# mLSTM cell and leaky-ReLU MLP on one core: the first weight matrix loaded slot by slot, onto 128 partitions at a time

## The chip, the cores and the metric

The kernel runs on one core of a Trainium2 chip. The metric is device time in microseconds (us) of one execution of the whole program. Inputs lie in the chip's memory (HBM) at the start, and the output has to be there at the end. The core has a matrix engine (PE, with PEld for the weight loads that overlap it), a vector engine (DVE), an activation engine (ACT), GpSimd (POOL) and a sync engine (SP). Each works through its own list of instructions in order, and they wait for one another on semaphores. Sixteen DMA engines move data between HBM and the on-chip memory (SBUF, 128 partitions); loads are issued from the queues of SP and ACT.

## The reference

Two stages. The first is an mLSTM cell with gates over 4 batches, 8 heads, 768 time steps and a head size of 40; the second is an MLP with a leaky ReLU on its 3072 rows of 320 numbers:

```python
for t in range(S):
    m_new = np.maximum(f_gate[:, :, t] + m, i_gate[:, :, t])
    f_stab = np.exp(f_gate[:, :, t] + m - m_new)
    i_stab = np.exp(i_gate[:, :, t] - m_new)
    C = f_stab[:, :, None, None] * C + i_stab[:, :, None, None] * np.einsum('bhd,bhe->bhde', vt, kt)
    n = f_stab[:, :, None] * n + i_stab[:, :, None] * kt
    h_tilde = np.einsum('bhde,bhe->bhd', C, qt)
    y[:, :, t] = o * h_tilde / np.maximum(np.abs((n * qt).sum(-1)), 1.0)[:, :, None]
...
x = attn_out.transpose(0, 2, 1, 3).reshape(B * S, H * D)   # 3072 x 320
h = x @ w_in                                               # 320 x 2048
return np.maximum(0.01 * h, h) @ w_out                     # 2048 x 320
```

(The line of `y` joins three of the reference's.) The two weight matrices are 64-bit floating-point numbers, so a row of w_in is 2048 x 8 = 16 KB in HBM, and 256 of its columns are 2 KB. Everything else is 32-bit.

## The kernel before, in words

**Chunks and units.** Time is cut into 6 chunks of 128 steps. For each chunk there are four steps, one for each batch, numbered `s` (0 to 3 are chunk 0). The cell of a chunk is worked out on all engines and gives x transposed (`xT`); the MLP of that chunk is cut into units (`ff_units`) that are laid between the cell's units of the next chunk. The orders of PE, DVE, ACT and POOL are written out by hand (`tc.manual_schedule`); SP's order is left to a scheduler.

**Chunk 0.** `first_chunk` issues the first loads and works through the cell of chunk 0. Then the main loop runs over the 32 units of chunk 0's MLP (`i` counts them) with the cell of chunk 1 between them. The first 16 units (L763, tile `ph`) multiply with w_in, the other 16 (L785, tile `po`) with w_out. The first eight of them use quarters 0 and 1 of w_in, the next eight quarters 2 and 3.

**w_in in SBUF.** The 320 rows of w_in are five blocks of 64, and its 2048 columns are four quarters of 512. A quarter (`n`) holds two sets of 256 columns, `r` = 0 and 1. Set 0 lies on partitions 0 to 63, set 1 on partitions 64 to 127, so that two matmuls of 64 rows can stand side by side. On each half the five blocks stand in five slots of 256 columns, in an order of its own:

```python
SLOTS = ([0, 2, 4, 1, 3], [1, 3, 0, 2, 4])
```

so slot 0 holds block 0 on the lower half and block 1 on the upper half, slot 1 blocks 2 and 3, slot 2 blocks 4 and 0, slot 3 blocks 1 and 2, slot 4 blocks 3 and 4.

**Loading and narrowing.** `load_weights(n)` loads quarter `n` as raw 64-bit words (L234): quarters 0 and 1 into the tail of the tile `acts`, 2 and 3 into the tile `raw`. For `n` of 4 and more it loads a pair of w_out's row blocks (L241). `narrow_weights(n)` then turns the words into 32-bit numbers in six steps: two on ACT (L253, L254) and four on DVE (L255, L258, L261, L262). L253 is the first to read the raw words. A quarter is usable when L262 has run.

Before, a quarter is loaded by four transfers. `run_of` finds the runs of slots whose blocks are two apart: three and two slots on the lower half, two and three on the upper. Each transfer writes 64 partitions, and its pattern has the 64 rows outermost, then two or three blocks, then 256 columns.

**What stands around the loads.** On SP's queue: k, q and v of steps 0 and 1 (L365), quarter 0, the output gates of steps 0 and 1, gates of chunk 2 (L94, L95), k and q of steps 2 and 3, quarter 1, v and output gates of steps 2 and 3, then a store to `a_dr` (L312), k and q for step 4 (L350, L377), quarters 2 and 3, v of step 4 (L354), and the tile `w` of step 4, two broadcast loads from `a_dr` (L407). Step 4 is the first of chunk 1. On it, POOL adds a mask to `w` (`prep_mask`, L446), POOL scales q (L483), ACT takes the exponent of `w` (`prep_exp`, L454), and PE turns the scaled q (`split_qs`, tile `tq`, L527) at unit 6 of the MLP. ACT's rows at L771 are the leaky ReLU of a unit; they free the PSUM banks that the unit wrote. From chunk 1 on, x goes through HBM: `u_mix` stores it to `x_dr` by four transfers of 20 partitions (L720), and `gather_x` loads it back (L734).

Every DMA announces its landing on one of eight semaphores, used in turn, and an issue waits for the earlier transfer on its semaphore.

Of the kernel before, what the change touches and what calls it, by code (L numbers as in the profile page):

```python
# [18 lines left out]
def kernel(  # L19
# [26 lines left out]
    nc = tc.nc  # L46
    B, H, S, D = q.shape
    P = 128
# [3 lines left out]
    Dm, FF = moe_w_in.shape  # L52
    PR = H // 2
    DP = 64
# [13 lines left out]
    KC = Dm // DP  # L68
    SLOTS = ([0, 2, 4, 1, 3], [1, 3, 0, 2, 4])
# [93 lines left out]
    QC = 4 * P  # L163
# [13 lines left out]
    def run_of(r, at):  # L177

        ks = SLOTS[r][at:]
        return ks[0], next((i for i in range(1, len(ks)) if ks[i] != ks[i - 1] + 2), len(ks))  # L180
# [11 lines left out]
    at = 3 * KH * NH  # L192
# [14 lines left out]
    def load_weights(n):  # L207

        m = n - QN
        if n < QN:  # L210
            dst = w_in[:, n, :]
        else:
            dst = w_out[:, 2 * m : 2 * m + 2, :].rearrange("p a d -> p (a d)")
        to = dst
        if wide:
            if n < 2:
                at = NF * GT - 2 * WC * (n + 1)
                raw = acts_l[:, at : at + 2 * WC].bitcast(U64)
            elif n < QN:
                raw = raw_t[:, WC * (n - 2) : WC * (n - 1)]  # L220
            elif m < 2:
                raw = w_out[:].rearrange("p f d -> p (f d)")[:, (2 + m) * WC : (3 + m) * WC].bitcast(U64)
            else:
                at = (4, 0, 1, 2, 3, 4)[m - 2] * HW
                raw = raw_t[:, at : at + HW]
            raws[n] = (raw, dst)
            to = raw
        if n < QN:
            src = moe_w_in[:, n * QC : (n + 1) * QC].rearrange("(k p) (r c) -> r p k c", p=DP, r=2)
            for r in range(2):  # L230
                at = 0
                while at < KC:
                    k0, n_k = run_of(r, at)
                    nc.sync.dma_start(  # L234
                        to[DP * r : DP * (r + 1), 2 * P * at : 2 * P * (at + n_k)].rearrange("p (k c) -> p k c", k=n_k),
                        src[r, :, k0 : k0 + 2 * n_k - 1 : 2, :],
                    )
                    at += n_k
        else:
            rows = moe_w_out[2 * m * P : 2 * (m + 1) * P, :]  # L240
            nc.sync.dma_start(to.rearrange("p (a d) -> p a d", d=Dm), rows.rearrange("(a p) d -> p a d", p=P))  # L241
# [842 lines left out]
    def first_chunk():  # L1084

        for n in range(2):
            for i in range(3):
                load_first(n, i)
        load_weights(0)
        for n in range(2):  # L1090
            load_first(n, 3)
        load_fi(2)
        for n in range(2, B):
            for i in range(2):
                load_first(n, i)
        load_weights(1)
        for i in (2, 3):
            for n in range(2, B):
# [83 lines left out]
    with tc.manual_schedule(engines={E.PE, E.DVE, E.Activation, E.Pool}):  # L1182
        ffs = first_chunk()
        feed(B, (0,))
        load_late(B, 1)
        load_weights(2)
        load_weights(3)
        feed(B, (1, 2))
# [131 lines left out]
```

## Time and profile before

| what | value |
|---|---|
| runs of the kernel | 502.24, 499.05, 498.44 us; median 499.05 |
| the profiled execution | 498.8 us, of it 497.0 us span (first to last instruction) |
| PE busy | 481.3 us, 97% of the span |
| PEld, DVE, ACT, POOL busy | 87%, 67%, 41%, 38% |
| mean granted clock of the matrix engine | 0.973 |
| DMA | 59.31 MB in 164912 packets, mean 119 GB/s |
| queue q1 (SP's) | 51.23 MB, 48.0% of the time of 16 engines |
| loads of w_in | 16 issues by SP between 8.0 and 42.7 us, 384 or 256 KB each |
| first matmuls with w_in (L763) | at 33.9 us |

The span is the time between the first and the last instruction of the profiled execution; its own time is 1.8 us longer. Busy time is the union of an engine's instructions. PE is busy in 97% of the span, but not in every stage: in the first 54 us it has gaps, and the DMA engines are busy for nearly all of the first 50 us.

### The profile page before, as it was taken

How to read it: one execution, taken by the hardware profiler on the slowest of the kernel's cores; microseconds unless marked ns; L12 is line 12 of the kernel's file. 1: busy time of each engine (PE TensorE's matmuls, PEld its weight loads, DVE VectorE, ACT ScalarE, POOL GpSimd, SP SyncE). 2: the span in 40 equal slices, each digit the busy share in tenths (PEclk: the TensorE clock that was granted, in tenths of full speed). 3: DMA queues.
4: the chain of work that ended last, by engine and by line, in shares of the span. 5: the costliest groups of instructions: out<-in, count | busy, mean ns of one | idle time of the engine just before them, and what ended most of it. 6: DMA issues, size and time to landing. Idle time of an engine off the chain costs nothing.

```text
span 497.0 us, 14017 instructions
## 1 busy us (share of the span) xinstructions
PE 481.3 (97%) x5651; PEld 432.1 (87%) x5651; DVE 331.2 (67%) x565; ACT 206.2 (41%) x500; POOL 190.3 (38%) x239
## 2 busy tenths in 40 slices
PE   8679899999999999999999999999999999999997
PEld 7659688877678879998899998899989899988997
DVE  5636658779947977886877786787836788104541
ACT  4545298774434461154631235720345611053210
POOL 4151414435345772495411694203583003700020
PEclk9758799999999999999999999999999999999999
DMA  9999885978750394486664586674766212200001
GB/s 119 168 176 199 128 210 110 266 135 178 162 138 8 95 187 89 115 173 149 148 139 106 136 163 134 156 141 89 161 145 142 61 54 54 80 1 1 0 1 54
DMA packets 164912, 59.31 MB, mean 119 GB/s; under 512 B 128432, under 2 KB 155632, under 8 KB 164848
## 3 DMA queue, kind: packets, MB, share of 16 engines
q1 hardware_dynamic: 124816, 51.23, 48.0%
q10 hardware_dynamic: 40032, 7.18, 9.3%
q8 instruction: 45, 0.74, 0.7%
q14 instruction: 19, 0.16, 0.1%
HBM read 51.68 MB, written 6.70 MB: 117 GB/s over the span
## 4 chain that ended last, share of the span: by engine, by line
PE 91%; DMA 2%; DVE 2%; SPq 1%; ACT 1%; issue 1%; POOL 1%; DVEq 0%; POOLq 0%
PE ph L936 32%; PE po L820 31%; PE po L785 7%; PE ph L763 7%; PE pT L699 3%; PE sd L622 3%; DMA raw<-in_moe_w_in_dram 2%; PE pa L645 1%; SPq L234 1%; PE sd L627 1%; PE hN L669 1%; PE warm L321 1%; PE tk L541 1%; ACT w L454 1%; PE tq L527 1%
## 5 line engine op out<-in xcount | busy, mean ns | idle before, releaser
L820 PE MATMUL po<-w_out,acts 128*128 128x160 f32 x640 | 89.1, 300 | 0.0
L820 PEld LDWEIGHTS po<-w_out,acts 128*128 128x128 f32 x640 | 87.3, 190 | 0.6 <-ACT acts L961 0.3
L936 PE MATMUL ph<-xT,w_in 64*128 64x256 f32 x720 | 83.4, 378 | 0.0
L936 PEld LDWEIGHTS ph<-xT,w_in 64*128 64x128 f32 x720 | 69.4, 187 | 9.4 <-issue 1.1
L820 PE MATMUL po<-raw,acts 128*128 128x160 f32 x480 | 66.4, 300 | 0.0
L820 PEld LDWEIGHTS po<-raw,acts 128*128 128x128 f32 x480 | 65.4, 190 | 0.3
L965 DVE TENSOR_TENSOR acts<-acts,ph 128x512 f32<-128x512 f32 x60 | 38.3, 681 | 40.0 <-PE ph L936 40.0
L599 POOL TENSOR_TENSOR S<-S,f 40x336 f32<-40x336 f32 x36 | 29.5, 819 | 81.5 <-PE pT L699 35.6
L454 ACT ACTIVATE w<-w,gT 128x64 f32<-128x64 f32 (+1 forms) x192 | 52.0, 348 | 12.7 <-POOL vu L474 4.6
L969 ACT COPY acts<-ph 128x512 f32<-128x512 f32 x60 | 32.1, 587 | 47.3 <-PE ph L936 47.3
L961 ACT ACTIVATE acts<-acts 128x1024 f32<-128x1024 f32 x30 | 31.7, 1056 | 38.1 <-DVE acts L965 35.9
L632 DVE TENSOR_TENSOR qn<-w,sd 64x512 f32<-64x512 f32 x40 | 27.3, 684 | 23.6 <-PE sd L627 10.3
L763 PE MATMUL ph<-xT,w_in 64*128 64x256 f32 x320 | 39.0, 398 | 2.0 <-DVE w_in L262 2.0
L446 POOL TENSOR_TENSOR w<-w,i 128x512 f32<-128x512 f32 x20 | 27.2, 1370 | 28.4 <-DMA w<-a_dr 19.3
L763 PEld LDWEIGHTS ph<-xT,w_in 64*128 64x128 f32 x320 | 32.1, 197 | 6.7 <-DVE w_in L262 2.2
L936 PE MATMUL ph<-acts,w 64*128 64x256 f32 x320 | 37.4, 381 | 0.0
L785 PE MATMUL po<-w_out,acts 128*128 128x320 f32 x128 | 37.1, 441 | 0.0
L713 POOL TENSOR_TENSOR xb<-xb,den 128x320 f32<-128x320 f32 x16 | 11.6, 727 | 60.8 <-DVE xb L710 60.8
L936 PEld LDWEIGHTS ph<-acts,w 64*128 64x128 f32 x320 | 30.9, 187 | 4.0 <-issue 0.4
L785 PEld LDWEIGHTS po<-w_out,acts 128*128 128x128 f32 x128 | 23.5, 190 | 9.9 <-issue 1.0
L853 POOL TENSOR_TENSOR y<-y,raw 128x160 f32<-128x160 f32 x10 | 9.5, 949 | 55.6 <-ACT y L852 54.7
L517 DVE TENSOR_TENSOR qn<-kqT,ea 64x512 f32<-64x512 f32 x32 | 28.6, 894 | 0.8
(164 smaller groups left out, 783.8 us busy)
## 6 DMA issues: line engine op xcount, KB each, us to landing
rb<-in_k_dram SPq DMA_DIRECT2D x64, 80.0 KB
rb<-in_q_dram SPq DMA_DIRECT2D x64, 80.0 KB
rb<-in_o_gate_dram SPq DMA_DIRECT2D x64, 80.0 KB
ea<-a_dr SPq DMA_DIRECT2D x32, 128.0 KB
raw<-in_moe_w_out_dram SPq DMA_DIRECT2D x6, 640.0 KB
w<-a_dr ACTq DMA_DIRECT2D x24, 128.0 KB
xT<-x_dr SPq DMA_DIRECT2D x32, 96.0 KB
x_dr<-x SPq DMA_DIRECT2D x64, 40.0 KB
```

What stands on the lines that cost most here:

```text
L446: nc.gpsimd.tensor_tensor(w, w, cm2.unsqueeze(1).to_broadcast([P, H, SL]), op=ALU.add)
L454: yield nc.scalar.activation(w[:, h, :], w[:, h, :], AF.Exp, bias=gT[c][:, 0, bh : bh + 1], scale=1.0)
L517: nc.vector.tensor_tensor(mixed(s)[rows, 1 - r], d["kqT"][rows, 1].rearrange("p (h t) -> p h t", t=SL), d["ea"][rows], op=ALU.mult,)
L599: nc.gpsimd.tensor_tensor(new, old, g, op=ALU.mult)
L632: nc.vector.tensor_tensor(mixed(s)[toks, u], w[toks], bank[1 - u][toks], op=ALU.mult)
L763: nc.tensor.matmul(ph[r][:, cols], lhsT=w_row(r, slot, j), rhs=xT[DP * r : DP * (r + 1), slot, cols], start=(slot == 0), stop=(slot == KC ...
L785: nc.tensor.matmul(po[n][:], lhsT=acts[:, f, ts(n, P)], rhs=w_out[:, f, :], start=(f == 0), stop=(f == NF - 1),)
L820: nc.tensor.matmul(bank[:], lhsT=left[:, f, :], rhs=right[:, f, :], start=f == 0, stop=f == KH - 1)
L936: nc.tensor.matmul(bank[r][:, e, :], lhsT=left(r)[rows, e], rhs=right(r)[rows], start=first and e == 0 and m == 0, stop=e == 1 and m == le ...
L961: nc.scalar.activation(to, z, AF.Prelu, alpha=0.01)
L965: nc.vector.tensor_tensor(to[:, 2 * r : 2 * r + 2], to[:, 2 * r : 2 * r + 2], bank[r], op=ALU.add)
L969: nc.scalar.copy(to[:, 2 * r : 2 * r + 2], bank[r])
```

## The change

A quarter of w_in is loaded slot by slot. For each slot the two blocks' addresses are worked out, `low` for set 0 and `high` for set 1. Where `high` is above `low` (slots 0, 1, 3 and 4), one transfer fills all 128 partitions of the slot: its source pattern is written by hand with three dimensions, 2 sets (at the distance `high - low`), 64 rows, 256 columns; its destination is 128 partitions of 256 columns. Slot 2, where the upper half's block is the earlier one, is loaded by two transfers of 64 partitions. That makes six transfers for four, 24 for 16 over the four quarters. The same bytes go to the same places. The instructions of PE, DVE, ACT and POOL and their order are the same; in SP's queue the loads that the scheduler orders between about 80 and 115 us stand in another order.

```diff
         if n < QN:
-            src = moe_w_in[:, n * QC : (n + 1) * QC].rearrange("(k p) (r c) -> r p k c", p=DP, r=2)
-            for r in range(2):
-                at = 0
-                while at < KC:
-                    k0, n_k = run_of(r, at)
-                    nc.sync.dma_start(
-                        to[DP * r : DP * (r + 1), 2 * P * at : 2 * P * (at + n_k)].rearrange("p (k c) -> p k c", k=n_k),
-                        src[r, :, k0 : k0 + 2 * n_k - 1 : 2, :],
-                    )
-                    at += n_k
+            for slot in range(KC):
+                low, high = (SLOTS[r][slot] * DP * FF + n * QC + r * 2 * P for r in range(2))
+                cols = slice(2 * P * slot, 2 * P * (slot + 1))
+                if high > low:
+                    src = bass.AP(moe_w_in.tensor, low, [[high - low, 2], [FF, DP], [1, 2 * P]])
+                    nc.sync.dma_start(to[:, cols], src)
+                else:
+                    for r, at in enumerate((low, high)):
+                        src = bass.AP(moe_w_in.tensor, at, [[FF, DP], [1, 2 * P]])
+                        nc.sync.dma_start(to[ts(r, DP), cols], src)
```

(FF is 2048, DP 64, P 128, KC 5, QC 512.)

## The prediction

> **What bounds the kernel now.** I read the timelines of the first 75 us first, because the edit touches only four loads that are issued there, then the windows for the rate of the DMA engines, then the trace's semaphore events and packet records. The columns of a timeline are start and length in us, engine, line, operation, and in brackets the idle time before it with what ended it; "SPq" rows are DMA issues.
>
> ```profile
> 7.98 3.11 SPq L234 DMA_DIRECT2D acts<-in_moe_w_in_dram  x4
> 21.95 2.98 SPq L234 DMA_DIRECT2D acts<-in_moe_w_in_dram  x4
> 35.64 7.02 SPq L234 DMA_DIRECT2D raw<-in_moe_w_in_dram  x8
> 48.98 4.32 SPq L407 DMA_DIRECT2D w<-a_dr  x2
> ...
> 19.05 1.36 ACT L253 ACTIVATE w_in<-acts 128x1280 f32<-128x1280 f32 x1 [3.92 <-DMA acts<-in_moe_w_in_dram]
> 37.39 1.40 ACT L253 ACTIVATE w_in<-acts 128x1280 f32<-128x1280 f32 x1
> 61.17 1.39 ACT L253 ACTIVATE w_in<-raw 128x1280 f32<-128x1280 f32 x1
> 68.71 0.82 ACT L454 ACTIVATE w<-w,gT 128x64 f32<-128x64 f32 x3
> 70.10 1.37 ACT L253 ACTIVATE w_in<-raw 128x1280 f32<-128x1280 f32 x1
> ...
> 56.83 1.37 POOL L446 TENSOR_TENSOR w<-w,i 128x512 f32<-128x512 f32 x1 [4.69 <-DMA w<-a_dr]
> ...
> 54.64 10.27 PE L763 MATMUL ph<-xT,w_in 64*128 64x256 f32 x78
> 65.88 6.82 PE L763 MATMUL ph<-xT,w_in 64*128 64x256 f32 x60
> 72.62 1.04 PE L527 MATMUL tq<-ident,y 64*40 64x64 f32 x30
> ```
>
> The reader is to see four deadlines, one for each quarter of w_in: the L253 rows at 19.05, 37.39, 61.17 and 70.10 us. From the semaphore events the quarters land at 18.9, 33.0, 46.6 and 53.0 us. Quarter 0 is waited for (3.92 us idle); the others have 4.4, 14.6 and 17.1 us of slack. From 54 us on PE is fed without a gap, and it holds 91% of the chain of waits: what is lost by PE in the first 75 us is not won back later. (The chain names the landing of `raw` ahead of L261 at 51.05 us, but that instruction reads `acts`; it stands behind L752 on its own engine, so I don't count that link as a dependency.)
>
> ```profile
> core 0: us, PE busy (x) PEld busy (x) DVE busy (x) ACT busy (x) POOL busy (x), PEclk, DMA share, GB/s
> 12.00:16.00 4.00, 2.21 (x20) 2.01 (x20) 3.51 (x10) 3.13 (x10) 2.22 (x7) 1.00 1.07 215
> 39.00:40.00 1.00, 1.00 (x12) 0.91 (x10) 0.92 (x4) 1.00 (x5) 0.00 (x0) 1.00 0.65 193
> 66.00:68.00 2.00, 2.00 (x20) 1.80 (x22) 1.86 (x2) 1.97 (x5) 0.00 (x0) 1.00 1.02 394
> ```
>
> The last two columns are the share of 16 DMA engines' time and GB/s. At 12 to 16 us only w_in moves, at 66 to 68 us only w_out.
>
> **What decides: how many engines carry a transfer.** In the semaphore events the landing of a transfer shows as increments, 16 for loads whose outermost dimension is 32, 64 or 128 (a handful of 500 show fewer, with records missing). `x_dr<-x` (L720, outermost dimension 20 on both sides) shows 11 each time, for all 64, and in the purest bursts of it (at 163 and 167 us, four transfers each) never more than 10 of its 512-byte packets are under way at once. So a transfer goes over as many engines as share its outermost dimension evenly (10 for 20, plus one increment for the rest), and four in a row use the same ten, or more than ten packets would overlap. The new pair transfers have 2 x 64 x 256 at the source and 128 x 1 x 256 at the destination. Only 1 and 2 divide both: I expect two engines, the same two each time, and 64 rows of 2 KB on each.
>
> The Trainium skill ("DMA: Bandwidth & Descriptors", section "Why a DMA increments its semaphore by 16 and not by 1") states this as a rule: the largest count up to 16 that divides the slowest dimension of both patterns, on the lowest-numbered engines. The 11 increments agree with it, and by it the sum is the one below.
>
> **Price of a row.** 16 engines at 66 to 68 us: 394 / (16 x 1.02) = 24.1 GB/s, so 2048 bytes take 85 ns. At 12 to 16 us: 215 / (16 x 1.07) = 12.6 GB/s, 163 ns. The packet records say when w_in is which: at 39 us, where few of its packets are under way and to both halves of the partitions, most take 84 ns; with all 16 engines on one half, 165 ns. Two engines, each writing a half of its own, are nearest to the first: I take 85 and keep 163 as the upper end; nothing in the records is under 81.
>
> **The change, part by part.** PE, ACT, DVE and POOL keep every instruction in its order; SP issues 24 loads for 16. The 8 more at 0.61 us (the L234 rows) are 4.9 us of SP, hidden while two engines are behind.
>
> A pair transfer: 64 x 85 ns = 5.4 us on its two engines. A half transfer (slot 2, 64 rows over 16 engines): 4 rows, 0.34 us. A quarter: 4 x 5.44 + 2 x 0.34 = 22.4 us against 640 / 16 x 163 ns = 6.5 us now. The queue is first in, first out on each engine (landings stand in the order of issue), and every other load has a sixteenth of its rows on these two engines; so each load behind a quarter lands behind it. A 160 KB load costs an engine 1.25 us (kn and qn land 1.2 to 1.4 us apart). Each issue also waits for the eighth transfer before it (eight semaphores in turn); with six to eight transfers in flight that leaves the two engines no gap. On them:
>
> - Quarter 0 starts at 10.2 us (its first packets now), ends at 32.7, lands 0.9 us later (as now) at 33.6.
> - Six loads of 160 KB, 7.5 us: 40.3. Quarter 1 ends at 62.7, lands at 63.6.
> - Six more: 70.3. Quarter 2 lands at 93.6; quarter 3 behind it at 116.0.
> - `w<-a_dr` for the first step of chunk 1 stands behind quarter 3; now it lands 3.66 us after it (56.67 against 53.01): 119.7.
>
> Against the deadlines, each shift carried to the next, since all four engines run in order:
>
> - L253 of quarter 0: 19.05 to 33.6, +14.6.
> - Quarter 1: 37.39 + 14.6 = 52.0, waits to 63.6: +26.2.
> - Quarter 2: 61.17 + 26.2 = 87.4, waits to 93.6: +32.4.
> - POOL L446: 56.83 to 119.8, done at 121.2. ACT L454 reads that tile: 68.71 + 32.4 = 101.1, waits to 121.2: +52.5.
> - Quarter 3: 70.10 + 52.5 = 122.6, landed at 116.0: no wait.
> - w_out's first pair lands 13.9 us after quarter 3 now (66.9): 129.9, needed at 77.58 + 52.5 = 130.1: no wait.
>
> What queues behind ACT's L454 are the L771 rows that free the PSUM banks of two units; PE's L763 stops after them and tq (L527) with it, so PE takes the shift whole: 53 us. Two things I set at nothing. SP's later order is a scheduler's: between the loads of chunk 1 and 2 some `rb`, `ea`, `w` and w_out loads change places, `w<-a_dr` falling behind six to eight small issues of 0.4 to 0.9 us (0 to +3 us; POOL's slack covers it, as PE is then 53 us behind the old times). PE's clock after an idle stretch (0.66 at 55 to 60 us) may cost 1 to 3 us at the new waits.
>
> Sum: 498.8 (the profiled execution: span 497.0 and 1.8 around it) + 53 = **552 us**. The median of the runs shown is 499.05, 0.25 above that execution, so nothing is added for it.
>
> **Rivals.**
> 1. Two engines, but 163 ns a row. For it: w_in's own rows now; against: the 84 ns at 39 us. A quarter is 4 x 10.4 + 0.7 = 42.4 us; landings at about 53.5, 103, 153 and 196, `w` at 199.6, L454 at 201.1: +132, 631 us. At 100 ns it would be 4 x 256 x 15 ns = 15 us over the forecast, 568.
> 2. The other side: the split goes by the destination's 128 partitions, 16 engines carry each pair transfer, eight rows each. For it: every load with 128 partitions now shows 16 increments; against: in all of these the source's outermost dimension is 128 too. Both halves would be written at once, so rows near 85 ns: a quarter in 3.4 us for 6.5. Quarter 0 would be 3.1 us earlier, out of ACT's wait of 3.92; but DVE's L255 behind it starts at 23.02, after den (L639) and PE's pa, so at most 3 us, likelier 1, reach the end: 498 us, not slower. It decides if more than about 8 engines share a pair.
>    The Trainium skill (same page, section "Rules for kernel authors") advises one 128-partition transfer in place of two on disjoint halves, which is what this change does; by that alone the time is this rival's.
> 3. Two engines, but a milder stall: later transfers take another two, or the two catch up between quarters. Against: never more than ten packets of `x_dr`. If only quarters 0 and 1 hurt, +26: 525 us.
>
> **How the numbers follow.** The forecast (538 to 575, its own range) has 0.70; rival 1 and dearer rows (575 to 640) 0.12; rival 2 0.11; rival 3 0.07. The range takes the forecast with the near parts of rivals 1 and 3: 525 to 605. A difference under 1% can't be told from none here (the three runs span 498.44 to 502.24). Rival 2 is nearly all within 1%: faster 0.03, same 0.08, slower 0.89.
>
> **What would show it.** Three increments at the landing of a pair transfer (two engines and the rest) and not 16; a DMA share near 2/16 between 13 and 33 us; ACT's L253 idle for some 18 us before quarter 0 and 11 before quarter 1, POOL's L446 idle for some 50 us until `w<-a_dr`; quarter 3 landed near 116 us; from there on the same rows as now, 53 us later, PE's busy time still near 481 us. Sixteen increments, or quarter 0 landed before 22 us, makes the prediction wrong at its root; a landing of quarter 0 at 45 us or later makes the row's price wrong.

## The result, and the profile after

The changed kernel takes 562.31 us (median of four runs, 558.55 to 564.6) against 499.61 us for the kernel before beside it: a ratio of 1.124, with a 95% interval of 1.115 to 1.133. The profiled execution is the fastest of the four, 558.55 us with a span of 556.7 us; against that of before (498.8, span 497.0) the span is 59.7 us longer. The medians differ by 62.7 us; no profile shows the 3 us between the two, since only the fastest execution was profiled.

The timeline of after, where each of the four quarters' deadlines was shown for before (columns as there):

```profile
70.82 16.35 SPq L234 DMA_DIRECT2D raw<-in_moe_w_in_dram  x4
...
110.63 2.45 SPq L407 DMA_DIRECT2D w<-a_dr  x2
...
33.82 1.35 ACT L253 ACTIVATE w_in<-acts 128x1280 f32<-128x1280 f32 x1 [18.95 <-DMA acts<-in_moe_w_in_dram]
62.94 1.35 ACT L253 ACTIVATE w_in<-acts 128x1280 f32<-128x1280 f32 x1 [12.75 <-DMA acts<-in_moe_w_in_dram]
91.28 1.37 ACT L253 ACTIVATE w_in<-raw 128x1280 f32<-128x1280 f32 x1
117.89 0.83 ACT L454 ACTIVATE w<-w,gT 128x64 f32<-128x64 f32 x3 [18.98 <-POOL w L446]
119.28 1.36 ACT L253 ACTIVATE w_in<-raw 128x1280 f32<-128x1280 f32 x1
...
116.59 1.26 POOL L446 TENSOR_TENSOR w<-w,i 128x512 f32<-128x512 f32 x1 [35.43 <-DMA w<-a_dr]
...
119.17 4.50 PE L763 MATMUL ph<-xT,w_in 64*128 64x256 f32 x20 [18.60 <-ACT acts L771]
123.60 1.03 PE L527 MATMUL tq<-ident,y 64*40 64x64 f32 x30
```

Three stalls stand in brackets, each put down to a load: 18.95 us before quarter 0, 12.75 before quarter 1, and POOL's L446, which waits 35.43 us for `w<-a_dr` and hands 18.98 us on to ACT's L454 and 18.60 to PE. The L234 issues have become long too: the four that start at 70.82 us hold SP for 16.35 us. One of them (71.42 to 76.81 us) holds it for 5.4 us, where an L234 issue took 1.9 us at most before.

The windows of after, for a stretch in which only pair transfers move:

```profile
core 0: us, PE busy (x) PEld busy (x) DVE busy (x) ACT busy (x) POOL busy (x), PEclk, DMA share, GB/s
25.00:31.00 6.00, 0.00 (x0) 0.00 (x0) 0.00 (x0) 0.00 (x0) 0.00 (x0) 0.50 0.13 50
```

No compute engine does anything in these 6 us. The DMA share, 0.13, is two engines of sixteen, and 50 GB/s is 25 for each.

From the semaphore events: all 16 pair transfers of the four quarters land with 3 increments each, all 8 half transfers with 16. From the packet records at 25 to 31 us: 24 or 25 packets of 2 KB start in each us, their median 84 ns.

Where the shift against before stands, by the start of the same instruction in the two timelines:

| instruction | before, us | after, us | shift, us |
|---|---|---|---|
| ACT L253, quarter 0 | 19.05 | 33.82 | +14.8 |
| ACT L253, quarter 1 | 37.39 | 62.94 | +25.5 |
| ACT L253, quarter 2 | 61.17 | 91.28 | +30.1 |
| ACT L454, first of chunk 1 | 68.71 | 117.89 | +49.2 |
| ACT L771, the first once tq (L527) has run | 77.03 | 128.01 | +51.0 |
| ACT L547 of step 6 | 94.45 | 152.89 | +58.4 |
| ACT L547 of step 7 | 107.72 | 167.41 | +59.7 |

After the last row the shift stays within 59.5 to 59.7 to the end (PE's rows at 200, 300, 400 and 490 us of before): nothing is won back. The step from 51.0 to 58.4 belongs to a wait that the prediction had set at nothing. The timelines there, first the row of before, then those of after:

```profile
82.39 1.70 SPq L377 DMA_DIRECT2D rb<-in_q_dram  x1
...
141.49 1.64 SPq L393 DMA_DIRECT2D rb<-in_k_dram  x2
143.59 0.90 SPq L241 DMA_DIRECT2D raw<-in_moe_w_out_dram  x2
144.59 0.41 SPq L314 DMA_DIRECT2D a_dr<-bu  x1
145.11 0.67 SPq L377 DMA_DIRECT2D rb<-in_q_dram  x1
...
144.22 0.31 PE L541 MATMUL tk<-ident,kn 64*40 64x64 f32 x4
150.88 0.33 PE L541 MATMUL tk<-ident,rb 64*40 64x64 f32 x2 [6.35 <-DMA rb<-in_q_dram]
```

PE's transposes of step 6 read a q tile (`rb`). Before, it was issued at 82.39 us and landed at 86.36, 6.9 us ahead of its use at 93.25. After, the scheduler has put two k loads and two w_out loads ahead of it, which stood behind it before; it is issued at 145.11, lands at 150.83, and PE stands for 6.35 us.

The view of the waits of after names the same loads, and the two rows to which POOL's wait is handed on (columns: engine, tile and line, what it waited for; us in all, times, longest):

```profile
POOL w L446 <- DMA w<-a_dr: 47.8, 5, 35.4
ACT w_in L253 <- DMA acts<-in_moe_w_in_dram: 31.7, 2, 18.9
ACT w L454 <- POOL w L446: 19.0, 1, 19.0
PE ph L763 <- ACT acts L771: 18.6, 1, 18.6
PE tk L541 <- DMA rb<-in_q_dram: 6.8, 2, 6.3
```

### The profile page after: what moved, and what is told of

Same layout as the page of the kernel before. It is cut to its first block, busy times and chain, and to the rows that moved or that the text cites. A ratio compares the mean times of both kernels' runs of the same rounds, so it can differ in the third digit from the quotient of the medians.

```text
span 556.7 us, 14035 instructions
## 1 busy us (share of the span) xinstructions
PE 490.0 (88%) x5651; PEld 439.5 (79%) x5651; DVE 328.5 (59%) x565; ACT 206.2 (37%) x500; POOL 188.8 (34%) x239
## 4 chain that ended last, share of the span: by engine, by line
PE 68%; SPq 24%; DMA 3%; DVE 3%; issue 1%; POOL 0%; DVEq 0%; POOLq 0%
PE po L820 28%; PE ph L936 26%; SPq L234 7%; SPq L365 6%; PE po L785 6%; SPq L354 5%; SPq L238 3%; PE pT L699 3%; PE sd L622 2%; DMA rb<-in_q_dram 2%; SPq L407 1%; DVE qn L517 1%; PE sd L627 1%; SPq L241 1%; DMA fi<-in_f_gate_dram 1%
## 5 line engine op out<-in xcount | busy, mean ns | idle before, releaser
L936 PE MATMUL ph<-xT,w_in 64*128 64x256 f32 x720 | 82.7, 378 | 0.0
L936 PEld LDWEIGHTS ph<-xT,w_in 64*128 64x128 f32 x720 | 69.2, 187 | 8.9 <-issue 1.1
L820 PE MATMUL po<-raw,acts 128*128 128x160 f32 x480 | 66.4, 300 | 0.0
L454 ACT ACTIVATE w<-w,gT 128x64 f32<-128x64 f32 (+1 forms) x192 | 51.8, 348 | 34.2 <-POOL w L446 19.0
L763 PE MATMUL ph<-xT,w_in 64*128 64x256 f32 x320 | 43.2, 427 | 20.4 <-ACT acts L771 18.6
L763 PEld LDWEIGHTS ph<-xT,w_in 64*128 64x128 f32 x320 | 35.3, 215 | 26.4 <-ACT acts L771 19.0
L599 POOL TENSOR_TENSOR S<-S,f 40x336 f32<-40x336 f32 x36 | 29.3, 814 | 77.9 <-PE pT L699 35.4
L446 POOL TENSOR_TENSOR w<-w,i 128x512 f32<-128x512 f32 x20 | 26.0, 1308 | 60.5 <-DMA w<-a_dr 47.8
L961 ACT ACTIVATE acts<-acts 128x1024 f32<-128x1024 f32 x30 | 31.7, 1056 | 38.5 <-DVE acts L965 35.1
L632 DVE TENSOR_TENSOR qn<-w,sd 64x512 f32<-64x512 f32 x40 | 27.4, 684 | 26.8 <-PE sd L627 11.1
L255 DVE TENSOR_SCALAR w_in<-w_in 128x1280 f32<-128x1280 f32 x4 | 3.8, 955 | 52.8 <-ACT w_in L253 52.8
```

Of the source, the lines that this page charges most:

```text
L454: yield nc.scalar.activation(w[:, h, :], w[:, h, :], AF.Exp, bias=gT[c][:, 0, bh : bh + 1], scale=1.0)
L599: nc.gpsimd.tensor_tensor(new, old, g, op=ALU.mult)
L763: nc.tensor.matmul(ph[r][:, cols], lhsT=w_row(r, slot, j), rhs=xT[DP * r : DP * (r + 1), slot, cols], start=(slot == 0), stop=(slot == KC ...
L820: nc.tensor.matmul(bank[:], lhsT=left[:, f, :], rhs=right[:, f, :], start=f == 0, stop=f == KH - 1)
L936: nc.tensor.matmul(bank[r][:, e, :], lhsT=left(r)[rows, e], rhs=right(r)[rows], start=first and e == 0 and m == 0, stop=e == 1 and m == le ...
L961: nc.scalar.activation(to, z, AF.Prelu, alpha=0.01)
```

## The experiments

Two questions: is it really the number of engines that carries a transfer, and not the issues, the three-dimensional pattern or the 128 partitions; and how do the quarters and SP's later order add up to the 60 us. "Program order" below means that SP, too, follows the order in which the kernel's text issues its loads, in place of the scheduler's. The kernel before ran beside all eight kernels; its medians there were 499.46 us (for the halves, the cut after row 62 and the two in program order) and 498.66 us (for the other four).

### Slot by slot, but in halves

```diff
-                if high > low:
-                    src = bass.AP(moe_w_in.tensor, low, [[high - low, 2], [FF, DP], [1, 2 * P]])
-                    nc.sync.dma_start(to[:, cols], src)
-                else:
...
+                for r in range(2):
+                    at = SLOTS[r][slot] * DP * FF + n * QC + r * 2 * P
+                    src = bass.AP(moe_w_in.tensor, at, [[FF, DP], [1, 2 * P]])
+                    nc.sync.dma_start(to[ts(r, DP), cols], src)
```

(The diff is against the changed kernel: every slot is loaded as it loads slot 2.)

> A quarter is loaded slot by slot as in the changed kernel, but each slot by two transfers of 64 partitions: 10 for a quarter, 40 in all, no pair pattern; every other load keeps its place in SP's queue of the kernel before. Theory A (the two engines that carry a pair transfer are the cause): each transfer has 64 rows outermost on both sides, shows 16 increments and puts 4 rows on each engine; a quarter is bound by its ten issues of 0.61 us, 6.1 us, or by 6.5 us of rows as before; landings within 2 us of before (18.9, 33.0, 46.6, 53.0), the time 498 to 504 us. Rival B (more and smaller issues on SP are the cause: 8 more cost 62 us): 24 more cost more than the change, above 570 us.

Measured: 500.53 us, ratio 1.002 (1.000 to 1.004), with 40 transfers in place of 16 or 24. All land with 16 increments. So neither the slots nor the number of issues costs more than 2 us; the pair transfers do. The windows of this kernel, where before had a share of 1.07 and 215 GB/s:

```profile
core 0: us, PE busy (x) PEld busy (x) DVE busy (x) ACT busy (x) POOL busy (x), PEclk, DMA share, GB/s
12.00:16.00 4.00, 2.22 (x20) 2.01 (x20) 3.43 (x10) 3.05 (x10) 2.23 (x7) 1.00 0.80 237
```

More bytes in less engine time: transfers to the lower and the upper half of the partitions now alternate, and the packets' median falls to 84 to 106 ns in each us from 12 to 16 (165 before). The quarters land at 17.2, 30.6, 42.9 and 50.2 us, 1.7 to 3.7 us earlier than before, more than the 2 us that were expected at most. In this kernel's timeline (its lines are four lower) the gain is gone at the second L249:

```profile
17.26 1.36 ACT L249 ACTIVATE w_in<-acts 128x1280 f32<-128x1280 f32 x1 [2.21 <-DMA raw<-in_o_gate_dram]
37.40 1.40 ACT L249 ACTIVATE w_in<-acts 128x1280 f32<-128x1280 f32 x1
```

The first starts 1.79 us earlier than before's 19.05, the second at 37.40 against 37.39. Landings that are 2 to 4 us earlier are worth nothing here.

### The old transfers, cut after row 62

```diff
-                    nc.sync.dma_start(
-                        to[DP * r : DP * (r + 1), 2 * P * at : 2 * P * (at + n_k)].rearrange("p (k c) -> p k c", k=n_k),
-                        src[r, :, k0 : k0 + 2 * n_k - 1 : 2, :],
-                    )
+                    for p0, p1 in ((0, 62), (62, DP)):
+                        nc.sync.dma_start(
+                            to[DP * r + p0 : DP * r + p1, 2 * P * at : 2 * P * (at + n_k)].rearrange("p (k c) -> p k c", k=n_k),
+                            src[r, p0:p1, k0 : k0 + 2 * n_k - 1 : 2, :],
+                        )
```

(The diff is against the kernel before. SP's queue stands in program order, and its loads show that order.)

> The kernel before with its four transfers of a quarter each cut after the 62nd of 64 rows: 62 + 2, eight transfers for a quarter, 32 in all; no pair pattern, no 128-partition transfer. SP's queue stands in program order (as in the two kernels with that order). Theory A (a transfer goes over the largest number of engines up to 16 that divides the outermost dimension of both sides evenly): 62 and 2 both give two engines, 3 increments at the landing; 320 rows of 84 ns on each engine, 26.9 us for a quarter; landings near 38, 72, 106 and 134 us, the time about 570 to 590 us. Rival C (the three-dimensional pair pattern, or the write to 128 partitions, is what is slow): 498 to 510 us, 16 increments.

Measured: 587.56 us (585.51 to 588.29), ratio 1.176 (1.172 to 1.179), and 80 us over the kernel before in the same program order (507.41, below). Every w_in transfer lands with 3 increments; the quarters land at 38.5, 72.3, 104.6 and 131.3 us, `w<-a_dr` at 134.6. These are the patterns of before, on 62 and 2 rows of one half of the partitions, with no hand-written pattern and no transfer to 128 partitions. An outermost dimension of 62 or 2 rows is enough. The rows cost 84 ns here as well, although both engines write the same half; the 165 ns of before stand where sixteen engines write one half.

### Cut after row 56

The same edit with `((0, 56), (56, DP))`, again 32 transfers and program order.

> The kernel before with its four transfers of a quarter each cut after the 56th of 64 rows: 56 + 8, as many transfers as in the cut after 62; SP's queue in program order. Theory A (even division): 14 engines and 8, with 15 and 9 increments at the landing; at most 50 rows on an engine and quarter, 4 to 8 us; within 6 us of the kernel before with this order (507.4), 502 to 513 us. Rival G (cutting transfers, their number or the order of SP is what made the cut after 62 slow): near that one's 588 us.

Measured: 514.57 us (510.54 to 517.39), ratio 1.032 (1.024 to 1.040), 1.6 us over the upper end of what was expected. The transfers land with 15 increments (56 rows: 14 engines) and 9 (8 rows: 8 engines), each the engines and one more, as 3 is for two. The rows' median is back at 141 to 168 ns in each us from 12 to 15. Against 587.56 for the cut six rows further on, the same number of transfers and issues is 73 us cheaper. The count of engines is thus seen to follow the outermost dimension for 2, 8, 10 (the 11 of `x_dr`), 14 and 16 engines. Against the kernel before in program order (next) PE is about 1 us ahead from 60 to 160 us, so these loads cost nothing where they are read. The later chunks then run differently: 2.8 us ahead at 200 us, 2.0 behind at 300, 4.2 behind from 380 to the end in the profiled executions, 7.2 in the medians. What makes these later steps was not found.

### SP in program order, before and after

```diff
-    with tc.manual_schedule(engines={E.PE, E.DVE, E.Activation, E.Pool}):
+    with tc.manual_schedule(engines={E.PE, E.DVE, E.Activation, E.Pool, E.SP}):
```

> The kernel before with SP's queue in program order instead of the scheduler's (one engine more in the list of those whose order is by hand); its loads behind the quarters stand in another order than before. It is the base for the next kernel. All theories: 498 to 510 us; how much the order of SP's later queue is worth when no load is late.

> The changed kernel with SP's queue in program order: the same order as the kernel of this order without the change, but for the quarters. The change costs 60 us in the profiles, 51 of them by 125 us, the last 9 at PE's transposes of step 6, which wait for the load of q that the scheduler had moved behind four others. Theory D (those 9 us are the price of the scheduler's reordering): the difference to the kernel of this order without the change is 49 to 54 us. Rival E (they are the price of SP's loads being 60 us late, whatever their order): the difference is 57 to 63 us.

Measured: 507.41 us (505.55 to 508.52) for the kernel before, ratio 1.016 (1.012 to 1.019); 558.81 us (556.62 to 559.25) for the changed one. With one rule of order for both, the change costs 51.4 us. The timeline of the second of the two at step 6:

```profile
141.37 1.30 SPq L377 DMA_DIRECT2D rb<-in_q_dram  x1
142.77 1.04 SPq L241 DMA_DIRECT2D raw<-in_moe_w_out_dram  x2
...
145.09 0.25 PE L541 MATMUL tk<-ident,rb 64*40 64x64 f32 x2
```

The q tile is issued 3.7 us earlier than in the changed kernel, lands at 144.9, and PE doesn't wait; it comes 0.2 us after the landing. At ACT's L547 of step 7 this kernel is 7.9 us ahead of the changed one. Then it loses that again: program order has costs of its own in the later chunks, in the kernel before too, which falls behind its scheduled self by 1.1 us at 126 us, 2.9 at 243, 4.8 at 320 and 8.8 at 369. So the pair of kernels says that the four quarters' loads cost 51 us, and the timelines say where the other 9 of the profiled execution are: in the waits at steps 6 and 7. The scheduler's new order is not all that makes them. In program order the q tile lands 58.9 us later than without the change (86.04 to 144.91) and PE comes 50.7 later; the tile's slack of 8.3 us covers that by 0.2. The late queue uses up the slack in both, and the new order is what exceeds it.

### Only some of the quarters as pairs

`if n < 1:` and `if n >= 2:` around the new code, the old code for the rest; SP in program order, so the base is 507.41.

> Only quarter 0 is loaded as in the changed kernel (two engines for a pair); quarters 1 to 3 as before; SP in program order. Deadlines theory (each late landing stalls the first reader, and the stall is carried on whole; a quarter that has slack then adds nothing): quarter 0 lands at 33.8, quarter 1 near 48 against a need at 52, the others with slack: the stall of the changed kernel at quarter 0, 12 to 15 us, over the base of 507.4: 519 to 523 us. Rival H (the cost is shared out by bytes, a quarter of 51 us each, or is regained later): at most 513, or near 507.

Measured: 519.74 us (517.61 to 521.39), +12.3.

> Only quarters 2 and 3 are loaded as in the changed kernel; 0 and 1 as before; SP in program order. Deadlines theory: quarter 2 starts at 38.3 and lands at 61.5 (needed at 61.2), quarter 3 at 84, w of step 4 behind it at 87.7; ACT's exponent of that tile, at 69.8 in the base, waits to 89 and PE with it: +19 to +23 us over the base of 507.4, 526 to 531 us. Rival H (by bytes): +26 or more, 533 us and up; rival I (quarters 2 and 3 have 15 us of slack and hide): 507 to 512.

Measured: 529.13 us (525.91 to 529.62), +21.7. The timeline of the second (its lines are twelve higher) shows the stall that was predicted for `w`, with quarters 0 and 1 as before:

```profile
62.01 1.37 ACT L265 ACTIVATE w_in<-raw 128x1280 f32<-128x1280 f32 x1 [1.00 <-DMA raw<-in_moe_w_in_dram]
88.56 0.82 ACT L466 ACTIVATE w<-w,gT 128x64 f32<-128x64 f32 x3 [19.62 <-POOL w L458]
```

Quarter 2 lands at 61.8 us, almost in time, quarter 3 at 83.7 and `w` behind it at 87.0; ACT's exponent stands for 19.62 us. Quarter 0 alone makes 12.3 us, quarters 2 and 3 alone 21.7. The remaining 17.4 of the 51.4 are what quarter 1 adds between them, by subtraction; quarter 1 alone was not run.

### w ahead of quarters 2 and 3

The changed kernel in program order, with the loads of v and `w` for step 4 (`feed(B, (1, 2))`) moved ahead of `load_weights(2)`.

> The changed kernel with SP in program order, and the loads of v and of w for step 4 issued ahead of quarters 2 and 3 instead of behind them. Theory A (at that point quarter 3's own landing is the next deadline, hardly earlier than w's): POOL's wait for w is gone, quarter 2 and 3 land 2 to 4 us later (near 94 and 116), ACT waits for quarter 3 instead (needed at 99): 554 to 559 us for 558.8. Rival F (the wait for w is a cost of its own, 19 us at the exponent): 538 to 545.

Measured: 559.79 us (558.24 to 562.29), against 558.81 without the move, and 0.8 us over the upper end of what was expected. In the timeline ACT's L454 no longer waits, and L253 does:

```profile
95.10 1.35 ACT L253 ACTIVATE w_in<-raw 128x1280 f32<-128x1280 f32 x1 [4.34 <-DMA raw<-in_moe_w_in_dram]
101.87 0.83 ACT L454 ACTIVATE w<-w,gT 128x64 f32<-128x64 f32 x3
117.37 1.35 ACT L253 ACTIVATE w_in<-raw 128x1280 f32<-128x1280 f32 x1 [13.99 <-DMA raw<-in_moe_w_in_dram]
```

`w` lands at 73.1 us and the exponent runs 16 us earlier than in the changed kernel, but quarter 3, now landing at 117.2, is read at 117.37. The two engines have some 84 us of pairs to carry (16 at 5.2 to 5.3), whichever load stands last. The stall at `w` is not a matter of the order of issue.

## Why the prediction was right, and where it was off

**The number of engines.** Three increments were predicted for a pair and came in all 16 cases. The cut after row 62 has the same 3 with neither of the pair's other marks, and the halves have 16 and no loss. That two engines are the cause is shown, and the rival in which 128 partitions bring 16 engines is out. Its second half, a gain of up to 3 us from earlier landings, is not borne out either: with 16 engines and quarter 0 landed 1.8 us earlier the end gains nothing (500.53 against 499.46). A landing 3.1 us earlier, as that rival had it, was not run.

The Trainium skill ("DMA: Bandwidth & Descriptors", section "Rules for kernel authors") says that two transfers on disjoint halves of the partitions share their engines and recommends one transfer on 128 in their place. Here the two halves take 500.53 us and the one transfer 562.31. The same table also says to put a dimension that is a multiple of 16 outermost, and that is the rule that decides: the pair's source has a 2 there.

**The price of a row.** Predicted 85 ns, 163 as the upper end; 84 measured. A pair lands 5.2 to 5.3 us after the pair right before it (5.44 predicted), a whole quarter behind another 22.0 us (90.65 to 112.69; 22.4 predicted). The rival with 163 ns is out, by the changed kernel and by the cut at 62.

**Landings and deadlines.** Predicted 33.6, 63.6, 93.6, 116.0 and `w` at 119.7; measured 33.7, 62.7, 90.7, 112.7 and 116.4. The 3.3 us at the end of the queue come in the main from the six other loads between two quarters, put at 7.5 us each time: quarter 1 landed 29.0 us after quarter 0 and quarter 2 28.0 after quarter 1, which less the 22.0 of a quarter leaves 7.0 and 6.0. The rest is the 0.4 us by which each quarter was priced too high. The shifts follow: +14.6 predicted and +14.8 measured at quarter 0, +26.2 and +25.5 at quarter 1, +32.4 and +30.1 at quarter 2, +52.5 and +49.2 at L454. Quarter 3 had no wait, as predicted.

At quarter 2 the near agreement is luck. It had come 0.6 us ahead of L253, so it had no wait, where 6.2 us were predicted; what took the shift from 25.5 to 30.1 was PE's clock. Behind the wait for quarter 1 the same rows run slower, first before, then after:

```profile
40.96 1.16 PE L567 MATMUL sc<-kqT 40*128 40x128 f32 x16
42.05 1.98 PE L645 MATMUL pa<-S,w 128*128 128x41 f32 x16
...
66.45 2.08 PE L567 MATMUL sc<-kqT 40*128 40x128 f32 x16 [12.69 <-ACT kqT L558]
68.46 3.63 PE L645 MATMUL pa<-S,w 128*128 128x41 f32 x16
```

The granted clock was 0.50 from 66.4 to 83 us, with PE busy for 15.1 of these 16.6 us, against 0.75 in the same stretch before (40.9 to 54.3 us), and PE's shift grew from 25.5 to 29.9 us by 85.2 us. L454 starts when `w` has landed and L446 has run, so this does not change the end.

POOL's wait for `w` was 35.4 us where some 50 were named as a sign: part of it went to an earlier wait of POOL, 18.6 us for v at L464, and only the time at which L446 ends (117.9, for 121.2) enters the sum.

By parts: quarter 0 alone moves ACT's L253 by 14.1 us (19.68 to 33.81, both in program order), but PE by 11.1 from 60 to 200 us, and the end by 12.3; what adds the last 1.1 us was not found. In the changed kernel too the 14.8 us shrink to 12.3 at ACT's L751, where before had 3.8 us of idle time. The prediction carried 14.6 on whole, which did no harm because quarter 1 was late in any case.

**SP's later order: the mis-sized term.** The prediction set it at nothing, 0 to +3 us, on the ground that POOL's slack would cover it, with PE 53 us behind the old times. That ground holds for a load whose issue time stays where it was. SP's queue was itself late by the same stall: the q tile of step 6 was issued 62.7 us later than before (82.39 to 145.11) and landed 64.5 us later, while PE came 51 us later; 13.5 us of difference less 6.9 us of slack are 6.6, the wait to within 0.3 us (6.35 in the timeline). Of the 62.7 us, SP's gate load (L94) ahead of it is already 59.65 late (79.36 to 139.01), so the new order adds 3.07; a landing that takes 1.8 us longer (3.97 to 5.72 from the issue) adds the rest of the 64.5. Together with a second, smaller wait at step 7 it is worth 8.7 us (51.0 to 59.7 in the table of shifts); in program order it is absent. The sum as it came out: PE starts again at +48.9 after the wait for `w`, 2.1 for the clock (below), 8.7 for the later order, 59.7 in all. The forecast had 53, 0 and 0. Its stalls were some 4 us too dear, which the clock half made up by luck, and the later order was the error that counts.

**The clock.** Put at 1 to 3 us and not added. What of it reaches the end is seen at the wait for `w`: PE's rows of L763 start again at 119.17 us with a shift of 48.9 and are at 51.0 when tq (L527) starts, and the windows show why:

```profile
119.00:123.60 4.60, 4.43 (x21) 4.09 (x21) 1.66 (x2) 4.60 (x12) 2.43 (x3) 0.55 0.88 145
```

After 18.6 us without work the granted clock (the number behind POOL's) is 0.55; the same matmuls had 1.00 before (70.3 to 72.6 us). That is 2.1 us, and another 1.1 are in the later term (6.35 us of wait at step 6, 7.5 us of shift). The 4.4 us behind quarter 1's wait go into the next wait. The page of the profile after:

```profile
PE 490.0 (88%) x5651; PEld 439.5 (79%) x5651; DVE 328.5 (59%) x565; ACT 206.2 (37%) x500; POOL 188.8 (34%) x239
PEclk9657558659799999999999999999999999999999
L763 PE MATMUL ph<-xT,w_in 64*128 64x256 f32 x320 | 43.2, 427 | 20.4 <-ACT acts L771 18.6
```

The mean L763 takes 427 ns against 398 before, and PE's busy time grew by 8.7 us, where "still near 481" was named as a sign: that sign was wrong.

**The third rival**, a milder stall at 525 us, is out: the pairs of quarters 2 and 3 land at the same distance as those of quarter 0, and alone they make 21.7 us. The end is 10.3 us over the forecast by the medians, 6.6 over by the profiled execution; the changed kernel's runs spread more (558.55 to 564.6) than those of before, and the profiled one is their fastest. What spreads them was not found.

## What to carry to other kernels

Before two transfers are merged, look at the outermost dimension on both sides: the number of increments at a landing, less one if it is under 16, tells how many engines carry it (3, 9, 11 and 15 increments for 2, 8, 10 and 14 engines here), and a dimension of 2 there turns sixteen engines into two, however many partitions are written. On a queue whose loads land in the order of issue, as this one's do, such a transfer delays everything issued behind it, so its price is found by following each later load to its first reader, not by its own deadline alone. And where a scheduler orders the queue, a changed number of loads changes later order too: compare each moved load's issue time with the new time of its reader, both of them shifted.

## What the runs showed of the hardware

A 2 KB row into one half of the partitions costs an engine some 165 ns when all sixteen engines write that half (medians of 151 to 168 in each us from 12 to 16 before), 84 ns when two do (the cut after row 62), and a median of 84 to 106 ns when transfers to both halves alternate on sixteen. The Trainium skill ("SBUF — State Buffer", section "Door 1: The DMA port swizzle") gives a reason: partitions 0 to 63 reach only 8 of the memory's 16 ports, with an asymptote of about 218 GB/s. Before's 215 GB/s agrees with that; the 50 GB/s of the pair transfers are far below it.

SP is held at an issue behind pair transfers for up to 7.3 us (23.01 to 30.34), and in the kernel cut after row 62 for up to 7.2 (55.32 to 62.55). The kernel before has two such issues too, of 6.2 us (12.43 to 18.59) and 6.1 (26.24 to 32.34), so it is not the two engines alone that hold it. What does was not isolated.

The granted clock is 0.50 in the stall before quarter 0 (25 to 31 us). Behind the stall before quarter 1 it stays at 0.50 from 58.3 to 89.0 us, although PE works for 15.1 of the 16.6 us from 66.4 on: an engine that the profile shows as busy can run at half its clock for long. Behind the stall of 18.6 us at `w` it is 0.55 for 4.6 us and costs PE 2.1 us more.
